# The last batch's ff stage by seven half-size products, with some masks and sums on GpSimd

## The chip, the cores and the metric

The kernel runs on one core of a Trainium2 chip. The metric is the device time of one execution in microseconds (us); lower is better. Its engines are called TensorE (PE in the profile, its weight loads PEld), VectorE (DVE), ScalarE (ACT), GpSimd (POOL) and SyncE (SP, which here issues DMAs). Each engine works through its own queue in order; semaphores order the engines among each other.

## The reference

Local attention with block summaries, then a feed-forward layer with a gelu.

```python
# q, k, v: (4, 8, 768, 64) float32; block, window = 32, 16
k_sum = k.reshape(B, H, nb, block, D).max(axis=3)
v_sum = v.reshape(B, H, nb, block, D).mean(axis=3)
scores_l = scale * q @ k^T, kept where |i - j| < window, else -1e9
scores_s = scale * q @ k_sum^T + log(block)
a = softmax(concat([scores_l, scores_s]))
attn = a @ concat([v, v_sum])
x = attn.transpose(0, 2, 1, 3).reshape(B * S, H * D)      # (3072, 512)
h = x @ w_in                                              # w_in (512, 2048)
g = h * sigmoid(1.702 * h)
out = g @ w_out                                           # w_out (2048, 512)
```

## The kernel before

The four batches go through the same stages one after the other, with the attention of a batch laid between the output products of the batch before. All matmuls are in bf16 or f16.

**Names of the order.** The whole program is one string, `ORDER` (lines 35 to 110): words with arguments, each of which calls one function (the table `ops`, line 915). A word's place sets the place of its instructions in the queue of each engine that it uses. An ending `.a`, `.d` or `.g` picks ScalarE, VectorE or GpSimd for it. `_Ordered` (line 18) wraps every engine and tells the framework after each instruction to keep it in program order; since all instructions go through it, the profile gives them all line 28.

**Attention of a batch.** `s.b.half.p` computes the scores of a half of the rows (half) and a pair of heads (p) into PSUM (`ps_s`), `e.half.p` takes the exponential on ScalarE (`a_sb`), `m.half.p` (`mask`, line 668) multiplies it by the 0/1 mask `mk` on VectorE, `v.b.half.p` multiplies it with the values (`ps_av`), `nn.half.g` normalises two pairs on VectorE (a reciprocal and a product into `x2`), and `d.half.g` turns the result by a DMA transpose on SyncE's queue into `xT` (`xTT[half][g]`). Before that, `xk` and `xq` turn keys and queries by DMA, `xa` and `ka`, `kR` fill in block maxima and halos of the keys, `vm` and `vb` sum the values by block (TensorE, then a copy and four additions on VectorE), `ha` and `sd` copy rows of values by DMA; `lk`, `lq`, `lv` load the next batch's inputs from GpSimd's queue. Batches alternate between two sets of buffers; set 0 (`kx0`, `qT0`, `vw0`, in the pool `even`) serves batches 0 and 2, set 1 batches 1 and 3.

**The ff stage.** `f.half.nt.k...` (`ff`, line 721) computes one ff tile: 128 of the 2048 ff columns for 384 of the batch's 768 rows, four matmuls over the model dimension of 512, into one PSUM bank `ph`; `g.half.nt` takes the gelu on ScalarE into `gT`. A batch has 16 x 2 such tiles.

**The output products.** They already go by seven products in place of eight (a Winograd form of Strassen's scheme): ff columns, rows and model columns are each cut in two, `ws` holds four sums of `w_out`, and `gs.j.n.what` (`g_sums`, line 740) forms four sums of `gT`, for `n` ff tiles from tile `j` on and their partners eight tiles on. `p.t.what` (`product`, line 829) is one product of eight matmuls of 256 columns, `what` in 1, 2, 6, 5, 7, 3, 4, into one of the banks `poA`, `poB`, `poC`; several of them accumulate into the same bank, and in between `x.t.what` (`taken`, line 852) copies the bank away (1, 6, 5, as `s`) or adds it to such a copy (2, 3, 7) or copies it out (4), on ScalarE or VectorE. `o` stores `osb` from SyncE's queue, three buffers of it. A product of type 5 needs the sums `gs.j.n.0` of all eight j, types 6, 7 and 3 those of kinds 1, 2 and 3.

**PSUM.** Banks 0 to 3 are single; 4 and 5 are two banks wide, whose halves are written 40, 41, 50, 51 and which are taken whole as 42 and 52.

**The same for the ff stage, not in use.** `seven_pool`, `w_sum7`, `x_sum7`, `product7`, `taken7` and `gelu7` (lines 751 to 814) are there for the ff stage; the order before has only `P7.0` near its end, which closes the pool of set 0 and makes nothing.

Of the kernel before, what the change touches and what calls it, by code (L numbers as in the profile page):

```python
# [17 lines left out]
class _Ordered:  # L18


    def __init__(self, tc, eng):
        self._tc, self._eng = tc, eng

    def __getattr__(self, name):
        f = getattr(self._eng, name)

        def call(*a, **kw):
            r = f(*a, **kw)  # L28
            self._tc.keep_in_program_order(r)
            return r  # L30

        return call
# [46 lines left out]
v.2.0.3.51 m.1.2 p.1.2.2 m.1.1 lq.3.5 p.1.7 o.1.0.0.0.2 nn.0.0 x.1.2.a o.1.0.1.0.2 m.1.3 x.1.7.a p.1.3 nn.0.1 lv.3.3.1
lq.3.7 m.1.0 p.1.4 p.2.1.2 v.2.1.0.40 v.2.1.2.50 d.0.0 v.2.1.1.41 v.2.1.3.51 x.2.5.a x.2.1.d x.1.3.a lq.3.3 p.2.6  # L80
o.1.1.0.0.2 x.1.4.d d.0.1 p.2.3 nn.1.0 x.2.6.a p.2.7 nn.1.1 p.2.2.3 x.2.7.a x.2.2.a lv.3.4.0 d.1.0 lv.3.2.1 p.2.4
f.0.9.k01.3 x.2.3.a f.0.1.k01.0 G d.1.1 o.1.2.0.0.2 f.0.1.k23 f.0.8.k01.1 f.0.8.k23 f.0.9.k23 x.2.4.a f.0.0.k01.2
f.0.0.k23 lk.3.6 g.0.1 g.0.9 g.0.8 f.1.1.k0123.0 f.1.8.k0123.1 g.0.0 f.1.9.k0123.3 g.1.1 g.1.9 g.1.8 f.1.0.k0123.2
f.0.10.k0123.0 g.0.10 gate.2 g.1.0 gs.0.2.2 xk.1.1.0 f.1.2.k0123.1 gs.0.2.0.d gs.0.2.1 xk.1.0.1 f.1.10.k0123.3 g.1.2
o.1.1.1.0.2 g.1.10 lq.3.6 f.0.2.k0123.2 gs.0.2.3 lv.3.5.1 f.1.3.k0123.1 vm.3.52 g.1.3 xk.1.1.1 g.0.2 xk.1.0.0
o.1.2.1.0.2 f.0.13.k0123.0 f.0.3.k0123.2 f.1.11.k0123.3 f.0.12.k0123.1 g.0.3 g.0.13 g.1.11 xa.0.1 f.0.4.k0123.2 xq.1.1
f.1.12.k0123.3 lq.3.1 f.0.11.k0123.0 g.0.4 gs.2.2.2.g g.0.12 f.1.5.k0123.1 g.0.11 lq.3.2 vb xa.1.1 xq.1.0 f.0.5.k0123.2
g.1.5 g.1.12 ha.3.3.0 f.1.4.k0123.0 kR.1.d g.1.4 f.1.14.k0123.3 g.0.5 f.1.6.k0123.1 g.1.14 gs.2.2.0 ha.3.1.0
# [25 lines left out]
def kernel(  # L114
# [636 lines left out]
    def seven_pool(n):  # L751
        even.close()
        if not n:
            return
        p7 = ctx.enter_context(tc.tile_pool(name="seven", bufs=2, side="right", reuse_waits="tile"))
        seven["pool"] = p7
        seven["w"] = p7.tile([128, 4, 2, n * 128], F16, name="ws7", tag="ws7", bufs=1)
        seven["x"] = p7.tile([128, 4, 2, HALF], F16, name="xs7", tag="xs7", bufs=1)

    def w_sum7(what, j0, n, eng):  # L760
        c = slice(j0 * 128, (j0 + n) * 128)
        d = slice(d_ff // 2 + j0 * 128, d_ff // 2 + (j0 + n) * 128)
        a11, a12, a21, a22 = (w_in_sb[:, 0:2, c], w_in_sb[:, 2:4, c], w_in_sb[:, 0:2, d], w_in_sb[:, 2:4, d])
        w = seven["w"][:, :, :, c]
# [10 lines left out]
    def product7(j, what, where=None):  # L775
        c = slice(j * 128, j * 128 + 128)
        d = slice(d_ff // 2 + j * 128, d_ff // 2 + j * 128 + 128)
        w, x = seven["w"], seven["x"]
        lhs, rhs, name = {
            1: (w_in_sb[:, 0:2, c], xTT[0][0], "A"),  # L780
            2: (w_in_sb[:, 2:4, c], xTT[0][1], "C"),
            6: (w[:, 1, :, c], x[:, 1], "A"),
            5: (w[:, 0, :, c], x[:, 0], "B"),
            7: (w[:, 2, :, c], x[:, 2], "A"),
            3: (w[:, 3, :, c], xTT[1][1], "B"),
            4: (w_in_sb[:, 2:4, d], x[:, 3], "A")}[what]
        opens = where is not None
        if opens:
            seven[j, name] = bank(where, F32, "ph" + name)[:, 0:HALF]
# [174 lines left out]
```

## Time and profile before

| | |
|---|---|
| median of 3 runs | 212.25 (211.74 to 213.11) |
| the profiled execution | 211.7 |
| its span, first to last instruction | 210.0 |
| moved by DMA | 27.74 MB, 132 GB/s in the mean |
| granted TensorE clock | 0.996 |

A row of a timeline has the start in us, the time until its last instruction ends, engine, line, operation, output<-input, partitions x elements and type, and how many instructions are merged in it; in brackets stands how long the engine stood idle before and for what. A row of a grouped view has the count, the busy time in us, the mean of one instruction in ns, and behind the second bar the engine's idle time before these instructions and what ended most of it.

In these terms batch 2's attention runs from about 100.8 us, its ff stage from 123.1, batch 3's attention from 144.6, batch 3's ff stage from 167.1 and the last output products from 187.9.

### The profile page before, as it was taken

The page shows a single profiled execution, that of the slowest core. Times are in us where ns is not written, and L with a number is a line of the kernel's source. Part 1 is how long each engine was busy: PE and PEld are TensorE (multiplying, and loading weights), DVE is VectorE, ACT ScalarE, POOL GpSimd, SP SyncE. Part 2 cuts the span into 40 slices and gives each one's busy share as a digit, 9 for nine tenths or more (in the row PEclk, how much of TensorE's full clock was granted, in tenths as well). Part 3 has the DMA queues.
Part 4 walks back from the last instruction along what each step waited for, and adds up shares of the span by engine and source line. Part 5 has one row for each costly group of instructions (what it writes and reads, how often), then busy time and mean ns, then how long its engine had stood idle before and what let it go on. Part 6 is the DMA issues. An engine that isn't in the chain of part 4 may idle for free.

```text
span 210.0 us, 5880 instructions
## 1 busy us (share of the span) xinstructions
PE 200.4 (95%) x2440; PEld 145.8 (69%) x2440; DVE 130.8 (62%) x311; ACT 114.3 (54%) x227; POOL 109.1 (52%) x157
## 2 busy tenths in 40 slices
PE   7998798999999999999999999999999999999993
PEld 5656554667887886556788865657888865668882
DVE  5577873798997871168997822694888500166342
ACT  2473885659666736676764336567670157671100
POOL 7999972399982998448949422431000000863000
PEclk9999999999999999999999999999999999999998
DMA  4999999999999999999999999939215920000214
GB/s 67 162 166 189 209 213 221 182 144 122 99 134 199 156 177 183 130 126 141 148 166 204 142 227 180 187 29 169 50 53 139 160 105 0 0 3 0 100 53 150
DMA packets 96458, 27.74 MB, mean 132 GB/s; under 512 B 85024, under 2 KB 93488, under 8 KB 96432
## 3 DMA queue, kind: packets, MB, share of 16 engines
q0 software_dynamic: 70800, 13.64, 82.7%
q1 hardware_dynamic: 25632, 13.74, 33.2%
q8 instruction: 19, 0.31, 0.6%
q14 instruction: 7, 0.06, 0.1%
HBM read 27.26 MB, written 6.29 MB: 160 GB/s over the span
## 4 chain that ended last, share of the span: by engine, by line
PE 79%; POOL 12%; DMA 5%; issue 1%; DVE 1%; SPq 0%; POOLq 0%; DVEq 0%
PE ph L28 36%; PE poA L28 19%; PE poB L28 10%; PE poC L28 5%; PE ps_s L28 3%; PE ps_av L28 3%; DMA vw<-vw 2%; POOL mk L28 2%; DMA out_dram<-osb 2%; POOL v0n L28 2%; POOL w_in_sb L28 2%; POOL kb L28 2%; POOL kx L28 2%; POOL qb L28 1%; PE ps_t L28 1%
## 5 line engine op out<-in xcount | busy, mean ns | idle before, releaser
L28 PE MATMUL ph<-xT,w_in_sb 128*128 128x384 f16 x512 | 86.1, 326 | 0.4 <-DVE osb L28 0.4
L28 ACT ACTIVATE gT<-ph 128x384 f16<-128x384 f32 x128 | 56.1, 495 | 30.6 <-PE ph L28 29.9
L28 PEld LDWEIGHTS <-w_in_sb 128*128 128x128 f16 x512 | 49.2, 98 | 32.4 <-issue 0.9
L28 PEld LDWEIGHTS <-gs 128*128 128x128 f16 x384 | 36.5, 98 | 4.6
L28 DVE TENSOR_TENSOR gs<-gT 128x768 f16<-128x768 f16 (+1 forms) x36 | 17.5, 498 | 29.1 <-ACT gT L28 29.0
L28 POOL TENSOR_TENSOR gs<-gs,gT 128x768 f16<-128x768 f16 (+1 forms) x6 | 8.8, 1461 | 41.8 <-PE ph L28 32.7
L28 POOL DMA_DIRECT2D kb<-in_k_dram x28 | 23.1, 842 | 13.7 <-DMA w_out_sb<-in_moe_w_out_dram 6.4
L28 ACT ACTIVATE a_sb<-ps_s 128x768 bf16<-128x768 f32 x32 | 24.8, 808 | 9.5 <-PE ps_s L28 9.3
L28 PEld LDWEIGHTS <-gT 128*128 128x128 f16 x288 | 27.3, 98 | 3.6
L28 POOL DMA_DIRECT2D vw<-in_v_dram x36 | 25.7, 752 | 5.0 <-DMA w_out_sb<-in_moe_w_out_dram 1.7
L28 PE MATMUL poA<-ws,gs 128*128 128x256 f16 x192 | 24.8, 273 | 0.0
L28 POOL DMA_DIRECT2D qb<-in_q_dram x28 | 23.8, 867 | 1.8 <-issue 0.9
L28 DVE TENSOR_TENSOR a_sb<-a_sb,mk 128x768 bf16<-128x768 bf16 x28 | 14.7, 550 | 3.0 <-ACT a_sb L28 2.2
L28 DVE TENSOR_TENSOR x<-ps_av,rc 128x768 f16<-128x768 f32 (+1 forms) x18 | 15.6, 869 | 0.6
L28 ACT ACTIVATE s<-poA 128x256 f32<-128x256 f32 x14 | 5.4, 382 | 19.3 <-PE poA L28 18.6
L28 PE MATMUL poB<-ws,gs 128*128 128x256 f16 x96 | 12.5, 273 | 0.0
L28 PE MATMUL poC<-w_out_sb,gT 128*128 128x256 f16 x96 | 12.5, 273 | 0.0
L28 PE MATMUL poA<-w_out_sb,gT 128*128 128x256 f16 x96 | 12.4, 273 | 0.0
L28 PE MATMUL poB<-w_out_sb,gs 128*128 128x256 f16 x96 | 12.4, 273 | 0.0
L28 PE MATMUL poA<-ws,gT 128*128 128x256 f16 x96 | 12.3, 273 | 0.0
L28 DVE TENSOR_REDUCE ka<-kx 128x48 bf16<-128x1536 bf16 x4 | 7.0, 1750 | 7.4 <-DMA kx<-kb 7.4
L28 ACT ACT_TABLE_LOAD x8 | 10.3, 1283 | 0.9 <-PEq L948 0.8
(102 smaller groups left out, 219.0 us busy)
## 6 DMA issues: line engine op xcount, KB each, us to landing
out_dram<-osb SPq DMA_DIRECT2D x23, 256.0 KB, 2.9
kb<-in_k_dram POOLq DMA_DIRECT2D x24, 96.0 KB, 6.0
qb<-in_q_dram POOLq DMA_DIRECT2D x24, 96.0 KB, 5.0
vw<-in_v_dram POOLq DMA_DIRECT2D x36, 64.0 KB, 5.1
w_out_sb<-in_moe_w_out_dram POOLq DMA_DIRECT2D x4, 512.0 KB, 14.8
w_in_sb<-in_moe_w_in_dram POOLq DMA_DIRECT2D x3, 512.0 KB, 11.3
vw<-vs SPq DMA_DIRECT2D x6, 198.0 KB, 3.9
kb<-in_k_dram POOLq DMA_DIRECT2D x4, 192.0 KB, 4.4
```

The source lines that it names most:

```text
L28: r = f(*a, **kw)
```

## The change

**The order.** `ORDER` is another one from batch 2's attention on (line 75 before). The counts of attention words and of output products stay; their places change, and the engines of some: three masks of batch 2 (`m.1.0`, `m.0.2`, `m.1.2`) and four of batch 3 (`m.0.0`, `m.0.3`, `m.1.0`, `m.1.1`) go to GpSimd, the halos `ka.1` too; some `gs` sums go from one to the other of VectorE and GpSimd; some `x` between ScalarE and VectorE.

**The pins.** `_Ordered` also adds, for each instruction, a dependency without a semaphore on the one before it on that engine.

**Seven products in the last ff stage.** `P7.6.2` closes the pool of set 0 once batch 2's attention is done, and opens in its place one for six pairs of ff tiles, (2, 10) to (7, 15). `W.what.2.6.d` forms four sums of `w_in` (128 x 1536 each) on VectorE during batch 2's ff stage, `U.what` four of `xT` (128 x 768 each), three on GpSimd and one on VectorE. `P.j.what` is a product of two matmuls of 384 columns (`product7`). A pair has three PSUM banks: a wide one `phX` with halves l and r, which in the end hold the left and the right half of tile j, and a single one `phA` for products 6, 7 and 4. `S.j.what` (`taken7`) copies l to `phA` after product 1 and r to the SBUF tile `r7` after product 5; after product 6 it adds `phA` and `r7` into r, in PSUM, where product 3 goes on accumulating, and after product 7 it adds `phA` to `r7`. `H.j.0`, `H.j.1` and `H.j.2` (`gelu7`) take the gelu of `phX` (both halves), `phA` and `r7`. Pairs (0, 8) and (1, 9) stay with `f` and `g`.

`w_sum` gets an engine argument that the order does not use, and `taken` takes the tiles `s1` from the pool `snap` always, as it did before in effect.

```diff
@@ _Ordered
             self._tc.keep_in_program_order(r)
+            if self._last is not None:
+                self._tc.add_manual_dep(r.ins, self._last, mybir.DependencyInfo(
+                    mybir.DependencyClass.NoSync, mybir.DependencyReason.DATA), reason="program order")
+            self._last = r.ins.name
             return r
@@ ORDER, batch 2's attention
+p.2.5.1 p.0.1.2 e.0.1 gs.7.1.1 gs.7.1.3 ha.2.3.0 x.0.1.a p.0.5.3 gs.6.1.1 gs.6.1.2.g x.0.5.a p.0.6 gs.4.2.3 ha.2.1.0
...
+e.0.2 s.2.1.1.52 lv.3.3.0 s.2.1.0.42 x.0.7.a e.1.0 m.0.0 p.0.4 x.0.3.a lq.3.0 m.1.0.g p.1.1.3 e.1.1 m.0.2.g o.1.0.0.0.2
+s.2.1.2.42 m.0.1 xk.1.0.1 x.0.4.a lq.3.4 lv.3.0.0 e.1.2 x.1.1.d s.2.1.3.52 m.0.3 p.1.2.2 x.1.5.a v.2.0.0.40 v.2.0.1.41
+p.1.6 x.1.6.a x.1.2.a m.1.2.g nn.0.0 p.1.3 p.1.7 e.1.3 x.1.3.a lq.3.5 o.1.0.1.0.2 lv.3.3.1 p.2.1.2 x.1.7.a x.2.1.d
+v.2.1.0.40 v.2.0.2.50 lq.3.7 v.2.0.3.51 d.0.0 lq.3.3 x.2.5.a m.1.1 nn.0.1 p.1.4 p.2.6 v.2.1.1.41 m.1.3 x.2.6.d
+v.2.1.2.50 v.2.1.3.51 nn.1.0 x.1.4.a o.1.1.0.0.2 p.2.3 d.0.1 p.2.2.3 p.2.7 nn.1.1 x.2.2.a f.0.9.k01.3 x.2.3.a d.1.0
@@ ORDER, the end of batch 2's ff stage and batch 3's attention
+f.1.5.k0123.1 g.1.5 f.1.15.k0123.3 gs.0.2.1 f.0.13.k0123.0 xq.1.0 o.1.1.1.0.2 g.0.13 f.0.6.k0123.2 f.1.6.k0123.1
+gs.4.2.0 f.0.15.k0123.0 g.1.15 gs.4.2.1 g.1.6 f.1.14.k0123.3 g.0.15 g.0.6 f.1.7.k0123.1 g.1.14 f.0.14.k0123.0 ha.3.1.0
+g.1.7 g.0.14 vb W.1.2.6.d o.1.2.0.0.2 gs.2.2.0.g gs.2.2.2.g gs.2.2.1.d f.0.7.k0123.2 gs.4.2.3.g ha.3.0.0 W.3.2.6.d
+gs.2.2.3 gs.6.1.0 o.1.2.1.0.2 sd.3.1.0 gs.7.1.0 ha.3.3.0 p.0.5.1 g.0.7 X s.3.0.0.52 s.3.0.1.42 p.0.1.2 gs.4.2.2.g
+p.0.2.3 e.0.1 p.1.2.0 gs.7.1.1.d x.0.5.d x.0.1.a s.3.0.3.42 gs.6.1.1 e.0.0 s.3.1.0.52 x.0.2.a gs.7.1.3 p.0.6 p.1.1.3
+gs.0.2.3 gs.6.1.3 e.1.0 x.1.1.d gs.6.1.2.g sd.3.0.0 ha.3.2.0 gs.7.1.2 e.0.3 m.0.0.g s.3.0.2.52 s.3.1.1.42 x.0.6.a e.0.2
+e.1.1 m.0.3.g p.0.7 p.0.3 s.3.1.3.42 x.0.7.a m.1.0.g m.0.1 m.0.2 s.3.1.2.52 x.0.3.a e.1.2 p.0.4 m.1.1.g e.1.3 p.1.6
...
@@ ORDER, batch 3's ff stage
+x.1.7.a nn.1.1 d.1.0 p.2.5.1 d.1.1 U.0.g U.1.g p.2.6 p.1.4 f.0.1.k01.0 G x.2.6.a x.1.4.a o.2.1.0.0.2 x.2.5.a P.3.1.52
+f.0.1.k23 P.2.1.42 p.2.2.3 p.2.3 x.2.2.a p.2.7 x.2.3.a g.0.1 f.0.8.k01.1 f.0.8.k23 U.2.d P.2.5 P.3.5 g.0.8 S.3.5.a
+f.1.1.k0123.0 S.2.5.a x.2.7.a f.1.8.k0123.1 p.2.4 g.1.1 S.2.1.a.0 g.1.8 S.3.1.a.1 P.2.6 P.2.2 P.3.2 P.3.6 f.0.9.k01.3
+S.2.6.d P.2.3 P.2.7 S.3.6.d S.2.7.d P.3.3 U.3.g P.3.7 f.0.9.k23 P.2.4 S.3.7.d x.2.4.a H.2.0 H.3.0 P.4.1.42 P.4.5 H.2.1
...
@@ mask
-    def mask(half, p):
+    def mask(half, p, eng=dve):
         a = a_sb[half, p]
-        dve.tensor_mul(a, a, mk[:, half * TH:(half + 1) * TH, :].unsqueeze(1)
+        eng.tensor_mul(a, a, mk[:, half * TH:(half + 1) * TH, :].unsqueeze(1)
                        .to_broadcast([128, 2, TH, QT]))
@@ product7
+            1: (w_in_sb[:, 0:2, c], xTT[0][0], "l"),
+            2: (w_in_sb[:, 2:4, c], xTT[0][1], "l"),
+            6: (w[:, 1], x[:, 1], "A"),
+            5: (w[:, 0], x[:, 0], "r"),
+            7: (w[:, 2], x[:, 2], "A"),
+            3: (w[:, 3], xTT[1][1], "r"),
             4: (w_in_sb[:, 2:4, d], x[:, 3], "A")}[what]
+        if where is not None:
+            X = seven[j, "X"] = bank(where, F32, "phX")
+            seven[j, "l"], seven[j, "r"] = X[:, 0:HALF], X[:, 512:512 + HALF]
         for i in range(2):
+            pe.matmul(out=seven[j, name], lhsT=lhs[:, i], rhs=rhs[:, i], start=(what in (1, 5) and i == 0),
+                      stop=(i == 1), skip_group_check=True)
@@ taken7
+        if what == 1:
+            seven[j, "A"] = bank(where, F32, "phA")[:, 0:HALF]
+            copy(eng, seven[j, "A"], seven[j, "l"])
+        elif what == 5:
+            seven[j, "h"] = seven["pool"].tile([128, HALF], F32, name="r7", tag="r7", bufs=3)
+            copy(eng, seven[j, "h"], seven[j, "r"])
         else:
+            to = seven[j, "r"] if what == 6 else seven[j, "h"]
+            eng.tensor_tensor(out=to, in0=seven[j, "A"], in1=seven[j, "h"], op=ALU.add)
```

More of the change, by code (lines that the diff above doesn't have):

```diff
@@ L79 @@
[L79 to L88, printed above, removed]
@@ L786, in product7 @@
             4: (w_in_sb[:, 2:4, d], x[:, 3], "A")}[what]
-        opens = where is not None
-        if opens:
-            seven[j, name] = bank(where, F32, "ph" + name)[:, 0:HALF]
-        seven[j, "at", what] = ph = seven[j, name]
+        if where is not None:
+            X = seven[j, "X"] = bank(where, F32, "phX")
+            seven[j, "l"], seven[j, "r"] = X[:, 0:HALF], X[:, 512:512 + HALF]
         for i in range(2):
-            pe.matmul(out=ph, lhsT=lhs[:, i], rhs=rhs[:, i], start=(opens and i == 0), stop=(i == 1),
-                      skip_group_check=True)
```

98 lines of the change are left out of this document (38 added, 60 removed).

## The prediction, made before the changed kernel was run

> **What bounds the kernel now.** I read the page's busy table first, then TensorE's timeline, then the grouped costs of the other engines, then the stretches where VectorE and GpSimd run together.
>
> ```profile
> span 210.0 us, 5880 instructions
> ## 1 busy us (share of the span) xinstructions
> PE 200.4 (95%) x2440; PEld 145.8 (69%) x2440; DVE 130.8 (62%) x311; ACT 114.3 (54%) x227; POOL 109.1 (52%) x157
> ```
>
> ```profile
> 166.23 1.04 PE L28 MATMUL poA<-ws,gT 128*128 128x256 f16 x8
> 167.10 20.96 PE L28 MATMUL ph<-xT,w_in_sb 128*128 128x384 f16 x128
> 187.90 1.04 PE L28 MATMUL poA<-w_out_sb,gT 128*128 128x256 f16 x8
> 188.77 1.04 PE L28 MATMUL poB<-ws,gs 128*128 128x256 f16 x8
> ```
>
> ```profile
> 123.10 8.61 PE L28 MATMUL ph<-xT,w_in_sb 128*128 128x384 f16 x52 [0.41 <-DVE osb L28]
> 131.64 0.60 PE L28 MATMUL ps_vs<-vw,E 64*32 64x128 bf16 x48
> 132.18 12.52 PE L28 MATMUL ph<-xT,w_in_sb 128*128 128x384 f16 x76
> 144.63 0.52 PE L28 MATMUL ps_s<-qT,kx 64*128 64x64 bf16 x24
> ```
>
> TensorE bounds it: 200.4 of 210.0 us. The last batch's ff stage is one solid block, 128 matmuls from 167.10 to 187.90, no gap: 20.80 / 128 = 0.1625 us each, four to an ff tile, 0.65 us. A product is eight matmuls, 188.77 - 187.90 = 0.87 us. In the part of the program that the change reorders, the one wait of TensorE for data is the 0.41 us before 123.10. So the change can win at most the matmuls that it removes and that wait; any new wait of TensorE is paid in full, and this block has no slack of its own to hide one.
>
> **The matmuls.** A pair of ff tiles is 2 tiles x 2 halves x 4 = 16 matmuls; by seven products it is 7 x 2 = 14, of the same width. Six pairs: 12 fewer, 12 x 0.1625 = **1.95 us won**, all on the path.
>
> **The sums of weights and of x.** Four sums of w_in (128x1536, VectorE), four of x (128x768; three on GpSimd, one on VectorE).
>
> ```profile
> L28 DVE TENSOR_TENSOR vs<-ps_vs,vpart 32x128 bf16<-32x128 f32 x12 | 3.4, 285 | 0.2
> L28 DVE COPY s<-poB 128x256 f32<-128x256 f32 x8 | 3.4, 420 | 1.7 <-PE poB L28 1.7
> L28 DVE RECIPROCAL rc<-ps_av 128x12 f32<-128x12 f32 x14 | 3.2, 228 | 3.6 <-PE ps_av L28 3.2
> L28 DVE TENSOR_TENSOR ws<-w_out_sb,ws 128x1024 f16<-128x1024 f16 x4 | 2.8, 688 | 0.5 <-DMA w_out_sb<-in_moe_w_out_dram 0.5
> L28 DVE TENSOR_TENSOR ws<-w_out_sb 128x1024 f16<-128x1024 f16 x4 | 2.7, 686 | 1.9 <-DMA w_out_sb<-in_moe_w_out_dram 1.9
> L28 DVE TENSOR_TENSOR gs<-gT,gs 128x384 f16<-128x384 f16 x7 | 2.6, 372 | 0.0
> ```
>
> ```profile
> L28 DVE TENSOR_TENSOR a_sb<-a_sb,mk 128x768 bf16<-128x768 bf16 x8 | 4.2, 551 | 0.1
> L28 DVE TENSOR_TENSOR x<-ps_av,rc 128x768 f16<-128x768 f32 x4 | 3.8, 958 | 0.1
> ```
>
> ```profile
> L28 POOL TENSOR_TENSOR gs<-gT 128x768 f16<-128x768 f16 x3 | 4.8, 1633 | 0.0
> L28 POOL TENSOR_TENSOR gs<-gs,gT 128x768 f16<-128x768 f16 x2 | 3.6, 1788 | 32.7 <-PE ph L28 32.7
> L28 POOL TENSOR_TENSOR gs<-gs,gT 128x384 f16<-128x384 f16 x1 | 0.9, 912 | 2.1 <-DVE gs L28 2.1
> ```
>
> ```profile
> 130.05 1.03 DVE L28 TENSOR_TENSOR gs<-gT 128x768 f16<-128x768 f16 x2 [6.67 <-ACT gT L28]
> ```
>
> ```profile
> DMA to landing us min/median/max: 2.7/2.8/4.3
> ```
>
> From 0.55 us at 768 and 0.69 at 1024 columns a weight sum of 1536 is an estimated 0.96 us. W.0 and W.2 fall into batch 2's ff stage, where VectorE stands idle 6.67 us: nothing. W.1 and W.3 stand late there, just ahead of gs.6.1.0 and gs.7.1.0; see the first crossing below. U.0 waits for the transpose of x's second half (landing 2.8 us after issue, the last row, from the tile view of xT), behind nn.1.0 (about 1.2 us with its reciprocal), then takes up to 1.79 on GpSimd: 5.8 us after v.3.1.1. TensorE has six products, two ff tiles and two half products (6 x 0.87 + 4 x 0.325 + 2 x 0.325 = 7.2 us) between the last value product and P.2.5, which needs U.0. U.1 to U.3 have more work ahead of their readers. Nothing, with 1.4 us to spare.
>
> **The chain inside the new stage.** Each pair evacuates four times (S.1, S.5 copies; S.6, S.7 adds) and takes three gelus.
>
> ```profile
> 168.93 0.49 ACT L28 ACTIVATE gT<-ph 128x384 f16<-128x384 f32 x1 [1.24 <-PE ph L28]
> ```
>
> ```profile
> 183.55 1.79 ACT L28 ACTIVATE gT<-ph 128x384 f16<-128x384 f32 x4 [0.16 <-PE ph L28]
> ```
>
> ```profile
> 146.76 1.49 ACT L28 ACTIVATE a_sb<-ps_s 128x768 bf16<-128x768 f32 x2
> ```
>
> The first gelu starts 0.2 us after its tenth matmul's slot (167.10 + 1.63 = 168.73). Back to back a 384 gelu costs ScalarE 0.43 us, a 768 one 0.7. ScalarE gets 8 plain gelus, 6 wide, 12 single, 8 copies: 28 x 0.43 + 6 x 0.7 = 16.2 us in a stage of 116 x 0.1625 = 18.85: busy 86%, and in order. VectorE gets 4 copies and 12 adds, about 0.55 each by the 256-column row of 0.42 quoted below, half full. Walking the three generations of two pairs by hand, TensorE is ahead of its releaser mostly at P.3.6, P.5.6, P.7.6 and the openings after a wide gelu, by 0.1 to 0.2 us each: I take **0.7 us lost**. No row shows ScalarE or VectorE writing PSUM; from 0 (all covered) to 2.0 (each of the 24 evacuations 0.3 us longer than a write to SBUF, a quarter of it exposed at TensorE).
>
> **Work moved to GpSimd.** This is where I choose.
>
> ```profile
> 185.37 0.49 DVE L28 TENSOR_TENSOR gs<-gT 128x384 f16<-128x384 f16 x1 [6.01 <-ACT gT L28]
> 185.79 2.26 DVE L28 TENSOR_TENSOR gs<-gs,gT 128x768 f16<-128x768 f16 x2
> ```
>
> ```profile
> 180.82 4.83 POOL L28 TENSOR_TENSOR gs<-gT 128x768 f16<-128x768 f16 x3
> 185.61 1.76 POOL L28 TENSOR_TENSOR gs<-gs,gT 128x768 f16<-128x768 f16 x1
> ```
>
> ```profile
> 190.72 0.42 DVE L28 TENSOR_TENSOR osb<-poC,s 128x256 f32<-128x256 f32 x1 [1.02 <-PE poC L28]
> 191.06 0.49 DVE L28 TENSOR_TENSOR gs<-gT,gs 128x384 f16<-128x384 f16 x1
> ```
>
> ```profile
> 190.43 0.91 POOL L28 TENSOR_TENSOR gs<-gT,gs 128x384 f16<-128x384 f16 x1
> ```
>
> Two VectorE sums that take about 0.9 us alone took 2.26 from 185.79, while GpSimd's sum ran from 185.61 to 187.37. The one at 185.37 slipped in between two GpSimd sums; the next, issued before that one had ended, had to let GpSimd go first. So the two engines take turns on sums that read two SBUF operands, and the one that waits, waits out the other's whole instruction. The add at 190.72 reads PSUM and one SBUF operand: 0.42, its usual time, under the GpSimd sum from 190.43. Masks, g sums and weight sums are of the first kind; evacuations, normalisation and block sums are not.
>
> The Trainium skill has this as a rule: "SBUF — State Buffer", section "Who interferes with whom", calls the pair of ports that VectorE and GpSimd share an exclusive lock, which a two-SBUF-input VectorE instruction and a GpSimd instruction that reads SBUF hold in turn. By it alone, moving masks to GpSimd would free VectorE of little and could hold it 1.6 us at a time; the rows at 185.79 and 190.72 agree.
>
> A GpSimd mask has no row; by the sums of the same size it is 1.63 us against VectorE's 0.47 (0.55 less the overlap of neighbours). Four crossings:
>
> First, the end of batch 2's ff stage. The new order runs product p.0.5.1 straight after the last ff tile; it needs gs.6.1.0 and gs.7.1.0 by its seventh and eighth matmul, 0.66 and 0.76 us in. On VectorE these stand behind gs.4.2.0, gs.4.2.1, the block sums (five small operations of 0.285, 1.4 us), W.1, gs.2.2.1, W.3, gs.2.2.3. gs.4.2.0 waits for the gelu of f.1.5, nine ff tiles (5.85 us) before the product: it starts 5.1 us before it. Alone: 4 x 0.47 + 1.4 + 2 x 0.88 + 2 x 0.29 = 5.6 us, ready 0.5 us into the product: just in time. But GpSimd now has gs.4.2.3, gs.4.2.2 (1.63 or more each) and gs.6.1.2 (0.91) in the same 5 us. The first hides behind the block sums but for 0.3; taking turns, the others add 2.5. So 0 to 2.7 us; by the row at 185.79, with a turn sometimes missed, **2.0**.
>
> Second, batch 3's attention: p.0.7 needs gs.7.1.2, on VectorE behind gs.0.2.3, gs.6.1.3 and x.1.1, while m.0.0 and m.0.3 run on GpSimd. Alone it is ready 0.4 us ahead. One turn 1.63 - 0.4 = **1.2**; bounds 0 and 2.7 (two turns, part of the second hidden).
>
> Third, batch 2's attention: v.2.1.2 and v.2.1.3 wait for nn.0.1 and m.1.3, behind m.1.1, which meets m.1.2 on GpSimd. GpSimd's masks also stand behind the loads lq.3.0, lq.3.4 and lv.3.0.0, with one to two us in hand. 0 to 0.9, **0.3**: half a turn less the cover. Against it the 0.41 wait goes.
>
> ```profile
> 122.63 0.42 DVE L28 TENSOR_TENSOR osb<-poC,s 128x256 f32<-128x256 f32 x1 [1.16 <-DMA out_dram<-osb]
> ```
>
> It came from x.2.2 finding its output buffer still being stored, and the new order takes that buffer from an earlier store: **0.41 won**.
>
> Fourth, the g sums after the new stage, five on GpSimd beside VectorE's: 0 to 0.9, **0.4**; the second half of them meets evacuations, which do not cross.
>
> The key halos moved from VectorE to GpSimd (ka.1) come ahead of lq.3.1 and lq.3.2; the loads go out about as late as before and xq.1.0 keeps its margin. The pins I price at nothing: the rows above show the engines in the written order already.
>
> Sum: -1.95 - 0.41 + 0.7 + 2.0 + 1.2 + 0.3 + 0.4 = +2.24 us. The profiled execution took 211.7 (span 210.0 and 1.7 around it), the median is 212.25, within 0.3%. On the median: **214.5**; with one or two of the crossings nearer to their lower or upper bounds, 212.3 to 216.5.
>
> **Rivals.** Cover holds: VectorE reaches gs.7.1.0 no later than 0.76 us into p.0.5.1, because its queue is served back to back and GpSimd waits instead, or GpSimd did its sums earlier. Decided at that one place; every later crossing then is the same kind. For it: alone, each chain is ready in time; the masks leave VectorE, 7 x 0.47 = 3.3 us. Against: 0.2 us of slack, and the row at 185.79. Then -1.95 - 0.41 + 0.7 = -1.7: 210.6, faster.
>
> Every turn lost: the upper bounds, -2.36 + 0.7 + 2.7 + 2.7 + 0.9 + 0.9 = +5.5: 217.8. Against it, a wait at one crossing gives VectorE time to catch up for the next.
>
> The PSUM chain: no crossing costs, but the evacuations are long: -2.36 + 2.0 = -0.4: 211.9.
>
> **How the numbers follow.** A measurement tells about 1% from no change. My forecast 0.50 (of it 0.18 within 1%, that is under 214.4), cover holds 0.30 (0.08 of it under 210.1), every turn lost 0.12, PSUM chain 0.08 (half of it with some crossings; 0.05 within 1%). Faster 0.08, within 1% 0.22 + 0.18 + 0.05 = 0.45, slower 0.32 + 0.12 + 0.03 = 0.47. The range leaves out the lower half of the second case and a third of the third: 210.5 to 217.4.
>
> **What would show it.** The ff stage: 32 plain matmuls on ph and 84 on phX and phA, about 19.6 us with waits. Before the first poB of batch 3, a wait of TensorE put down to VectorE's gs, and VectorE's W sums or g sums at 1.5 us or more under a GpSimd sum. Before p.0.7 a second. GpSimd's masks at 1.6. Wrong: no wait of TensorE there, VectorE's sums at 0.55 with GpSimd's stretched instead; or waits inside the stage put down to ScalarE's phA.

## The result, and the profile after

The changed kernel takes 223.88 us in the median of four runs (223.53 to 224.67) against 212.0 (211.42 to 213.11) before: 1.056 times the time, 95% interval 1.051 to 1.061. Some executions of a kernel come out more than 1.5% longer than its fastest one; the medians in this document are over all runs, the ratios over the others alone. The direction was forecast, the size was not: 214.5, with 217.4 as the upper end. The profiled execution took 223.97, its span is 222.3 against 210.0.

First the head of the page and its rows of busy tenths for TensorE and its clock (the changed kernel):

```profile
span 222.3 us, 5934 instructions
## 1 busy us (share of the span) xinstructions
PE 203.7 (92%) x2428; PEld 145.1 (65%) x2428; DVE 143.3 (64%) x308; ACT 121.0 (54%) x239; POOL 133.0 (60%) x174
...
PE   7897899999999999998999769993999999998994
...
PEclk9999999999999999999999979999799999999999
```

Twelve matmuls fewer, and TensorE is busy 3.3 us longer: some of its matmuls have become slower. The row of the clock says which: two of its forty slices read 7, and each stands near a slice in which TensorE idles (the 7 and 6 and the 3 of the PE row). Next, TensorE's timeline of the changed kernel from batch 2's ff stage on; only rows that the account below uses:

```profile
126.42 0.50 PE L28 MATMUL ph<-xT,w_in_sb 128*128 128x384 f16 x2 [0.54 <-DMA xT<-x]
129.61 13.21 PE L28 MATMUL ph<-xT,w_in_sb 128*128 128x384 f16 x70 [2.69 <-DMA xT<-x]
...
149.79 0.82 PE L28 MATMUL poB<-ws,gs 128*128 128x256 f16 x6
154.02 0.55 PE L28 MATMUL poB<-ws,gs 128*128 128x256 f16 x2 [3.41 <-DVE gs L28]
...
156.92 2.44 PE L28 MATMUL poC<-w_out_sb,gT 128*128 128x256 f16 x16
159.29 0.52 PE L28 MATMUL ps_s<-qT,kx 64*128 64x64 bf16 x24
...
163.42 0.28 PE L28 MATMUL poA<-ws,gs 128*128 128x256 f16 x1 [0.42 <-DVE gs L28]
...
168.35 1.03 PE L28 MATMUL poA<-w_out_sb,gT 128*128 128x256 f16 x8 [0.35 <-ACT osb L28]
```

```profile
204.08 3.10 PE L28 MATMUL poA<-ws,gs 128*128 128x256 f16 x24 [0.63 <-DVE gs L28]
207.46 1.05 PE L28 MATMUL poB<-w_out_sb,gs 128*128 128x256 f16 x8 [0.29 <-DVE gs L28]
```

And the granted clock around the two large waits, by windows (stretch, its length, then busy time and count of PE, PEld, DVE, ACT and POOL, and behind them the clock, the DMA share and GB/s):

```profile
130.00:131.00 1.00, 1.00 (x7) 0.57 (x6) 0.00 (x0) 0.87 (x3) 0.85 (x2) 0.84 0.92 138
131.00:132.00 1.00, 1.00 (x4) 0.46 (x3) 0.00 (x0) 0.38 (x1) 0.68 (x1) 0.50 0.64 74
...
134.00:135.00 1.00, 1.00 (x7) 0.63 (x6) 0.00 (x0) 0.63 (x2) 0.00 (x0) 0.95 0.51 33
...
154.00:155.00 1.00, 0.98 (x22) 0.69 (x24) 0.86 (x3) 0.00 (x0) 0.00 (x0) 0.79 0.00 0
155.00:156.00 1.00, 1.00 (x16) 0.73 (x11) 0.42 (x2) 0.66 (x1) 0.00 (x0) 0.50 0.00 0
...
157.00:158.00 1.00, 1.00 (x7) 0.69 (x6) 0.00 (x0) 0.84 (x2) 0.00 (x0) 0.51 0.00 0
```

TensorE goes on at full clock when the wait ends (1.00 in the stretch from 129 to 130), and then falls to half of it: at 130.7 behind the first wait (a mean of 0.84 in the stretch from 130 is 0.32 us at half) and at 154.6 behind the second, 1.1 and 0.6 us after TensorE went on. By the stretches in which it returns (0.95 and 0.51) it is back at 134.1 and 158.0: 3.4 us at half clock each time, which loses 1.7 us of work. The 70 matmuls from 129.61 took 13.14 us to the next row at 142.75 (not shown) where 70 x 0.1625 = 11.4 are due: 1.8 us beyond the wait itself. Between 154.02 and 159.29, 5.27 us went by with work for 3.3 (26 matmuls of 0.109 and one set of scores of 0.46): 2.0 beyond the wait. So of these 1.8 and 2.0 us the clock has 1.7 each.

The account by stages, each stage's length taken from where TensorE starts it, in us (products that the change has moved over a border are counted with their old stage, 0.87 each):

| stage | before | after | difference |
|---|---|---|---|
| up to batch 2's ff stage | 123.10 | 122.83 | -0.3 |
| batch 2's ff stage | 21.53 | 26.96 | +5.4 |
| batch 3's attention | 22.47 | 29.14 | +6.7 |
| batch 3's ff stage | 20.80 | 19.95 | -0.85 |
| last output products | 18.33 | 19.94 | +1.6 |
| behind the last product | 3.77 | 3.48 | -0.3 |
| span | 210.0 | 222.3 | +12.3 |

Of the 5.4, 3.2 are waits for `xT` and 1.8 is lost behind them, nearly all to the halved clock; of the 6.7, 3.4 are the wait inside p.0.5.1, 2.0 is lost behind it, 1.7 of that to the clock, and 0.8 are the next two waits. The rest are short lags.

### The profile page after: what moved, and what is told of

Same layout as the page of the kernel before. It is cut to its first block, busy times and chain, and to the rows that moved or that the text cites. A ratio compares the mean times of both kernels' runs of the same rounds, so it can differ in the third digit from the quotient of the medians.

```text
span 222.3 us, 5934 instructions
## 1 busy us (share of the span) xinstructions
PE 203.7 (92%) x2428; PEld 145.1 (65%) x2428; DVE 143.3 (64%) x308; ACT 121.0 (54%) x239; POOL 133.0 (60%) x174
## 5 line engine op out<-in xcount | busy, mean ns | idle before, releaser
L28 PE MATMUL ph<-xT,w_in_sb 128*128 128x384 f16 x416 | 74.2, 331 | 3.4 <-DMA xT<-x 3.2
L28 PEld LDWEIGHTS <-w_in_sb 128*128 128x128 f16 x452 | 43.8, 99 | 33.3 <-issue 6.1
L28 ACT ACTIVATE gT<-ph 128x384 f16<-128x384 f32 x104 | 46.3, 497 | 29.9 <-PE ph L28 28.7
L28 PEld LDWEIGHTS <-gs 128*128 128x128 f16 x384 | 36.2, 98 | 11.4 <-DVE gs L28 6.4
L28 PEld LDWEIGHTS <-gT 128*128 128x128 f16 x288 | 27.9, 100 | 5.1 <-issue 0.3
L28 POOL DMA_DIRECT2D kb<-in_k_dram x28 | 23.1, 840 | 11.4 <-DMA w_out_sb<-in_moe_w_out_dram 6.2
L28 POOL TENSOR_TENSOR gs<-gT 128x768 f16<-128x768 f16 (+1 forms) x8 | 12.6, 1578 | 14.4 <-ACT gT L28 14.4
L28 POOL TENSOR_TENSOR a_sb<-a_sb,mk 128x768 bf16<-128x768 bf16 x7 | 12.1, 1747 | 8.8 <-ACT a_sb L28 8.8
L28 DVE TENSOR_TENSOR a_sb<-a_sb,mk 128x768 bf16<-128x768 bf16 x21 | 13.4, 658 | 2.9 <-POOL mk L28 1.5
L28 PE MATMUL poA<-w_out_sb,gT 128*128 128x256 f16 x96 | 13.3, 285 | 0.3 <-ACT osb L28 0.3
L28 PE MATMUL poA<-ws,gT 128*128 128x256 f16 x96 | 12.3, 273 | 0.0
L28 DVE TENSOR_TENSOR gs<-gs,gT 128x768 f16<-128x768 f16 (+1 forms) x17 | 12.0, 721 | 0.2
```

## The experiments

Three theories came from this reading. **Loads:** GpSimd's masks of batch 2 hold up the loads behind them in its queue, these then run while the transposes `d` fetch x, and xT lands late. **Turns:** the wait in p.0.5.1 is VectorE's queue of sums held up by GpSimd's, as forecast; its rival is that W.1 and W.3 simply stand in the way. **Clock:** a wait of TensorE beyond some length costs the halved clock behind it as well; its rival is that what slows these matmuls is something else that happens there. Single times spread (the kernel before took 210.2 to 214.9 in 17 runs beside one group of these), so where a kernel was run once, its waits are read first and its time second.

### Loads

The answers of the tile xT, batch 2's four transposes, before and after, and GpSimd's timeline in the changed kernel:

```profile
DMA to landing us min/median/max: 3.2/4.3/5.7
```

```profile
DMA to landing us min/median/max: 5.8/6.1/7.8
```

```profile
109.72 3.55 POOL L28 TENSOR_TENSOR a_sb<-a_sb,mk 128x768 bf16<-128x768 bf16 x2 [1.39 <-ACT a_sb L28]
113.21 0.89 POOL L28 DMA_DIRECT2D qb<-in_q_dram  x1
114.10 0.70 POOL L28 DMA_DIRECT2D vw<-in_v_dram  x1
114.81 1.66 POOL L28 TENSOR_TENSOR a_sb<-a_sb,mk 128x768 bf16<-128x768 bf16 x1
...
120.95 0.87 POOL L28 DMA_DIRECT2D kb<-in_k_dram  x1
129.71 0.19 POOL L28 CAST gate<-xT 128x1 bf16<-128x1 f16 x1 [7.88 <-DMA xT<-x]
```

Three masks push the last loads out to 121.8; before, the last one ran from 116.74 to 117.6. The transposes are issued at the same times in both (113.9 to 121.7 and 114.0 to 121.3), but now share the time with loads and take 1.8 us longer in the median.

**m2_vector.** The changed kernel with batch 2's three masks back on VectorE.

```diff
-... lq.3.0 m.1.0.g p.1.1.3 e.1.1 m.0.2.g o.1.0.0.0.2
+... lq.3.0 m.1.0 p.1.1.3 e.1.1 m.0.2 o.1.0.0.0.2
...
-p.1.6 x.1.6.a x.1.2.a m.1.2.g nn.0.0
+p.1.6 x.1.6.a x.1.2.a m.1.2 nn.0.0
```

> The changed kernel with the three masks of batch 2 back on VectorE, all else as it is. Theory A: the masks hold up the input loads behind them on GpSimd's queue; the loads then share the DMA engines with the transposes of x, which land 5.8 us or more after issue (before: 4.3 in the median), so TensorE waits 3.2 us at the start of batch 2's ff stage and then runs at half its clock for some 3 us. It expects the loads 3 to 4 us earlier, landings of x at about 4.5, no wait over 0.5 us on xT there, no dip of the granted clock there, and a span 4.5 to 5.5 us shorter, 217 to 218. Rival B: the keys' transpose xk.1.0.1, moved early on SyncE's queue, and the stores delay x; it expects the wait and the dip unchanged and a span within 1 us of 222.3.

Measured 218.9, span 217.2, 5.1 shorter than the changed kernel's. The loads end at 115.6, the landing is below, no wait for xT is left and no halved clock there; the wait in p.0.5.1 is still 3.40.

```profile
DMA to landing us min/median/max: 2.8/4.1/7.6
```

This takes away masks and late loads together, so the next run takes the loads alone.

**loads_behind.** The masks stay on GpSimd; six loads that are issued among the transposes move behind the gate, where GpSimd waits for xT anyway.

```diff
-... lq.3.5 ... lv.3.3.1 ... lq.3.7 ... lq.3.3 ... lv.3.4.0 ... lv.3.2.1 ... gate.2 P7.6.2
+... gate.2 lq.3.5 lv.3.3.1 lq.3.7 lq.3.3 lv.3.4.0 lv.3.2.1 P7.6.2
```

> The changed kernel with its masks left on GpSimd, and the six loads lq.3.5, lv.3.3.1, lq.3.7, lq.3.3, lv.3.4.0, lv.3.2.1 moved behind the gate that waits for x. Theory A expects what the masks' removal gives at this place: landings of x at 3 to 4.5 us, no wait on xT over 0.5 us, no dip of the clock; the later loads may cost something at xq or at the block sums. Rival B expects the wait unchanged. Rival C, that the masks delay VectorE's normalisation through the shared port and not the loads, expects the wait unchanged too.

Measured 220.0, span 218.3, 4.0 shorter. Landing:

```profile
DMA to landing us min/median/max: 2.7/3.0/6.0
```

No wait for xT and no halved clock at the start of the stage. So it was the loads, not the masks as such. The wait in p.0.5.1 is 4.16 here, and the clock is halved for 6.8 us from within it (5.0 of them with work, so 2.5 lost in place of 1.7); these two make up for more than the 1.1 us that this kernel wins less than m2_vector.

How late xT lands is not a matter of the loads alone, though. Of the fourteen kernels of this document, five have loads beside the transposes until 121.5 or later; in all of them TensorE waits for xT at the start of the stage, 1.3 to 3.2 us. In seven of the other nine it doesn't, in no_crossing and best (below) it waits 1.1 and 1.4. The medians of the landing overlap: 5.2 to 8.1 us in the five, 3.0 to 5.9 in the nine.

**masks_alone.** The kernel before, with the same three masks on GpSimd and nothing else.

```diff
-m.0.2 ... m.1.2 ... m.1.0
+m.0.2.g ... m.1.2.g ... m.1.0.g
```

> The kernel before with only the three masks of batch 2 on GpSimd. Theory: in before's order the first of these masks comes later among the loads, two of them ahead of lq.3.5 and later loads; the loads go out about 3 us later, x lands later by 1 to 2 us and TensorE waits 1 to 3 us at the start of batch 2's ff stage, with a dip if it is over 2: 1 to 4 us more than before. Rival: masks on GpSimd are harmless by themselves and only the new order makes them costly; within 0.5 us of before.

Measured 214.91 in the median of four runs against 211.81 in the same round: 1.0147, interval 1.0091 to 1.0202. The masks alone cost some 3 us. Its profile shows two places. TensorE waits 1.27 us for xT; but the transposes are issued some 2.5 us later here than before (116.7 to 123.8), so this wait can't be put down to the loads alone. The cause of the delay is the second place, first TensorE, then VectorE, then GpSimd:

```profile
117.80 1.03 PE L28 MATMUL poA<-ws,gT 128*128 128x256 f16 x8 [1.87 <-DVE osb L28]
```

```profile
109.84 5.63 DVE L28 TENSOR_TENSOR a_sb<-a_sb,mk 128x768 bf16<-128x768 bf16 x1
```

```profile
110.73 1.66 POOL L28 TENSOR_TENSOR a_sb<-a_sb,mk 128x768 bf16<-128x768 bf16 x1
112.32 0.73 POOL L28 DMA_DIRECT2D vw<-in_v_dram  x1
113.06 1.65 POOL L28 TENSOR_TENSOR a_sb<-a_sb,mk 128x768 bf16<-128x768 bf16 x1
```

A mask of VectorE that takes 0.55 alone took 5.63: two GpSimd masks that started after it ended before it, and all that stands behind it on VectorE, the output adds among them, was late. In the changed kernel the VectorE mask in the same place got through in 0.76. These runs do not let one foresee which of the two happens.

### Turns

VectorE's and GpSimd's timelines of the changed kernel before p.0.5.1, from 145.26 and 143.16:

```profile
145.26 1.87 DVE L28 TENSOR_TENSOR gs<-gs,gT 128x768 f16<-128x768 f16 x1
...
148.58 1.15 DVE L28 TENSOR_TENSOR ws<-ws,w_in_sb 128x1536 f16<-128x1536 f16 x1
149.66 1.98 DVE L28 TENSOR_TENSOR gs<-gs,gT 128x768 f16<-128x768 f16 x1
151.57 1.66 DVE L28 TENSOR_TENSOR ws<-w_in_sb,ws 128x1536 f16<-128x1536 f16 x1
153.15 0.55 DVE L28 TENSOR_TENSOR gs<-gT,gs 128x768 f16<-128x768 f16 x1
```

```profile
143.16 3.56 POOL L28 TENSOR_TENSOR gs<-gT 128x768 f16<-128x768 f16 x2 [4.55 <-ACT gT L28]
147.28 1.64 POOL L28 TENSOR_TENSOR gs<-gT,gs 128x768 f16<-128x768 f16 x1 [0.56 <-DVE gs L28]
148.88 3.53 POOL L28 TENSOR_TENSOR gs<-gT 128x768 f16<-128x768 f16 x2
```

Each stretched VectorE sum ends just after a GpSimd sum does, and the first one after GpSimd's last sum takes 0.55 again. Against 0.55 for a sum and 0.96 for W (as g4_vector below shows it) the four stretched ones cost 1.32 + 0.19 + 1.43 + 0.70 = 3.6 us; TensorE's wait is 3.4.

**g4_vector.** The changed kernel with gs.4.2.3, gs.4.2.2 and gs.6.1.2, the three GpSimd sums that the first crossing was priced by, on VectorE and later, behind gs.7.1.3.

```diff
-f.0.7.k0123.2 gs.4.2.3.g ha.3.0.0 ... p.0.1.2 gs.4.2.2.g p.0.2.3 ... gs.7.1.3 p.0.6 ... x.1.1.d gs.6.1.2.g sd.3.0.0
+f.0.7.k0123.2 ha.3.0.0 ... p.0.1.2 p.0.2.3 ... gs.7.1.3 gs.4.2.2 gs.4.2.3 gs.6.1.2 p.0.6 ... x.1.1.d sd.3.0.0
```

> The changed kernel with W.1 and W.3 where they are, late, and only the three GpSimd g sums that met them (gs.4.2.3, gs.4.2.2, gs.6.1.2 of batch 2) moved to VectorE, behind gs.7.1.3 of batch 3's attention. VectorE's work ahead of p.0.5.1 is the same as in the change; what goes is the other engine. Theory of turns: the sums W.1, gs.2.2.1 and W.3, which took 1.15, 1.98 and 1.66 us, go back to about 0.95, 0.55 and 0.95; that is 2.3 us, the wait at p.0.5.1 falls from 3.4 to 0.8 to 1.4 us and the dip goes. Rival, that VectorE just has too much ahead of that product: the wait stays over 2.5 us.

Measured 222.97, span 221.3: only 1.0 won. TensorE's rows at the two crossings:

```profile
149.89 0.55 PE L28 MATMUL poB<-ws,gs 128*128 128x256 f16 x2 [1.06 <-DVE gs L28]
...
161.52 0.28 PE L28 MATMUL poA<-ws,gs 128*128 128x256 f16 x1 [4.26 <-DVE gs L28]
```

In front of p.0.5.1 the wait fell from 3.41 to 1.06, the W sums took 0.96 and 0.95, gs.2.2.1 0.56, and no halved clock followed. gs.4.2.1 still took 1.88, beside gs.2.2.0 and gs.2.2.2 on GpSimd, which the prediction had not counted. But the sums now stand on VectorE ahead of gs.7.1.2, and there they met batch 3's masks on GpSimd:

```profile
156.06 3.69 DVE L28 TENSOR_TENSOR gs<-gT,gs 128x768 f16<-128x768 f16 x2
```

So p.0.7 waits 4.26, and the half clock moved behind it. The turns are paid where two-input work of both engines meets, wherever that is put.

**w_early.** The changed kernel with W.1 and W.3 right behind W.2, where VectorE is idle.

```diff
-... W.2.2.6.d f.0.12.k0123.1 ... vb W.1.2.6.d o.1.2.0.0.2 ... ha.3.0.0 W.3.2.6.d gs.2.2.3
+... W.2.2.6.d W.1.2.6.d W.3.2.6.d f.0.12.k0123.1 ... vb o.1.2.0.0.2 ... ha.3.0.0 gs.2.2.3
```

> The changed kernel with W.1 and W.3 straight behind W.2, at the start of batch 2's ff stage, where VectorE is idle for 12 us. Theory: at p.0.5.1 the weight sums and the turns taken with GpSimd's g sums make TensorE wait 3.4 us; without the two, 2.8 us of VectorE's time (1.15 and 1.66, waits for GpSimd in them) leave the chain, the wait falls to 0.6 to 1.2 us, the clock does not dip behind it (2.0 us), and the span falls by 4 to 5 us to 217.5 to 218.5. Rival: GpSimd's sums only fall on the other g sums instead and the wait stays over 2.5 us with its dip; span within 1 us of 222.3. The wait on xT stays in both.

Measured 220.0, span 218.3, 4.0 shorter; the waits were

```profile
127.12 15.09 PE L28 MATMUL ph<-xT,w_in_sb 128*128 128x384 f16 x82 [2.88 <-DMA xT<-x]
151.68 0.55 PE L28 MATMUL poB<-ws,gs 128*128 128x256 f16 x2 [1.67 <-DVE gs L28]
```

The first has its halved clock, the second none. With the W sums out of the way 1.7 us of p.0.5.1's wait is gone, not the 1.15 + 1.66 that they took: GpSimd's sums still hold up two of VectorE's (1.88 and 1.87 in its timeline). Both theories have their share: the W sums in the path, and GpSimd's turns.

**m3_vector.** The changed kernel with batch 3's four masks on VectorE (`m.0.0`, `m.0.3`, `m.1.0`, `m.1.1`, without the ending `.g`).

> The changed kernel with the four masks of batch 3 back on VectorE, all else as it is. It prices the second crossing: 0.42 us before p.0.7 and 0.35 before v.3 in the changed kernel. Theory: both waits go, no more than 0.8 us of TensorE's time; the waits on xT and at p.0.5.1 stay with their dips. Rival: the masks hold up more than shows as waits; over 1.5 us less between 154 and 175 us.

Measured 222.84, span 221.1, 1.2 shorter: the waits of 0.42 at p.0.7 and 0.35 behind it are gone, p.0.5.1's is 3.41 as before. The second crossing was real and small.

### Clock

**wait_short** and **wait_long.** The kernel before, with one mask of batch 3 (0/1, so that repeating it changes nothing) done five and ten times on VectorE, to make TensorE wait where before it does not.

```diff
-p.0.4 p.1.7 m.1.0 x.0.4.a
+p.0.4 p.1.7 m.1.0 m.1.0 m.1.0 m.1.0 m.1.0 x.0.4.a
```

> The kernel before with the mask m.1.0 of batch 3 done five times over on VectorE (the mask is 0 or 1, so nothing changes in the result): 4 x 0.47 = 1.9 us more ahead of the normalisation nn.0.1 and of v.3.1.0. It measures what a wait of TensorE costs beyond its length. Theory: a wait of 1 to 1.5 us near 161 us, no dip of the granted clock behind it (no wait under 2 us has had one so far), and a span longer by the waits alone, 1 to 2 us. Rival: any wait dips the clock.

> The same with m.1.0 ten times: 9 x 0.47 = 4.2 us more. Theory: a wait of 3 to 3.6 us, then the granted clock at 0.5 for 3 to 3.5 us, which costs another 1.6 to 1.8 us; span 5 to 6 us longer than before. Rival: the dips after the waits of 2.7 and 3.4 us in the changed kernel have another cause (the DMA, or the kind of work); the clock stays at 1.0 here and the span grows by 3 to 4 us.

wait_short took 214.17, wait_long 218.06. TensorE's rows, first of the short, then of the long one, and the clock of the long one:

```profile
161.46 1.03 PE L28 MATMUL poB<-w_out_sb,gs 128*128 128x256 f16 x8 [1.11 <-DVE s L28]
162.33 1.04 PE L28 MATMUL poA<-ws,gT 128*128 128x256 f16 x8
```

```profile
163.23 1.87 PE L28 MATMUL poB<-w_out_sb,gs 128*128 128x256 f16 x8 [4.06 <-DVE s L28]
164.89 1.91 PE L28 MATMUL poA<-ws,gT 128*128 128x256 f16 x8
```

```profile
161.00:162.00 1.00, 0.00 (x0) 0.00 (x0) 0.93 (x4) 0.00 (x0) 0.00 (x0) 0.64 0.00 0
...
168.00:169.00 1.00, 1.00 (x18) 0.87 (x15) 0.67 (x2) 0.00 (x0) 0.00 (x0) 0.95 0.91 359
```

A wait alone does it, without seven products, masks on GpSimd or a DMA that is late. Behind the short one, products start every 0.87 us as ever; behind the long one, every 1.66. Here the clock falls within the wait, at 161.3, and is back at 168.1: 6.8 us, twice as long as in the changed kernel and as I had expected. 4.9 us of it had work, which cost 2.4. So the lengths are not all the same, and the price of a long wait is not one figure. (Both kernels' traces have a halved clock early on too, from 24.8 and 21.3 us; that is far ahead of the edit and plays no part in these rows.)

### What the seven products are worth

**hybrid.** The order of before up to batch 3's ff stage, with the four W sums in batch 2's ff stage, and the changed kernel's order from there.

```diff
 (the order before, to nn.1.1 of batch 3; in batch 2's ff stage:)
+P7.6.2 W.0.2.6.d W.2.2.6.d W.1.2.6.d W.3.2.6.d g.0.1
 (then the changed order:)
+d.1.0 d.1.1 U.0.g U.1.g f.0.1.k01.0 x.2.6.a o.2.1.0.0.2 x.2.5.a P.3.1.52 f.0.1.k23 P.2.1.42 ...
```

> The order of before up to batch 3's ff stage, masks on VectorE; all four weight sums at the start of batch 2's ff stage; from batch 3's ff stage on the order of the change, seven products with it. It shows what the seven products are worth alone. Theory: the ff stage at 19.6 to 20.0 us against 20.8, no wait on xT and none at the first product; behind the stage the g sums still cross, 1.0 to 1.6 us. Together minus 1.0 plus 1.3: 0.0 to 0.8 us more than before, 211.8 to 213.2. Rival: the seven products are themselves what costs (PSUM chains, sums of x), and the kernel stays over 216.

Ten runs, 212.84; ratio 1.0039 (0.9995 to 1.0083). In its profile, waits of 0.62 and 0.29 for g sums stand behind the new stage, as in the changed kernel: the fourth crossing. The stage itself, counted as in the table, takes 20.4 us here and in hybrid_sums, where 19.6 to 20.0 was expected: 0.4 less than the 20.80 before, which is too little for ten runs to tell. TensorE also waits 1.24 us for an `osb` at the start of batch 2's ff stage (0.41 before).

**hybrid_sums.** The same, with the four g sums of GpSimd behind the last ff pairs on VectorE, and the `x` copies that VectorE had there on ScalarE.

```diff
-gs.6.1.1.g ... gs.6.1.2.g ... x.0.6.d gs.7.1.3.g ... gs.6.1.3.g ... x.0.4.d ... x.1.6.d ... x.2.6.d
+gs.6.1.1 ... gs.6.1.2 ... x.0.6.a gs.7.1.3 ... gs.6.1.3 ... x.0.4.a ... x.1.6.a ... x.2.6.a
```

> As hybrid, but behind the last ff stage the four small g sums (gs.6.1.1, gs.6.1.2, gs.7.1.3, gs.6.1.3) on VectorE in place of GpSimd, and three copies of products on ScalarE in place of VectorE. Theory: the waits there (0.6, 0.4 and 0.3 us) come from turns with GpSimd; they fall under 0.4 together and the kernel gains 0.8 to 1.2 us on hybrid, 211.6 to 212.0. Rival: VectorE is simply full there; the four sums cost it 1.1 us more and the waits stay or grow, 212.8 or more.

Ten runs, 211.91 against 211.55: ratio 1.0008 (0.9972 to 1.0043). The two waits behind the stage are gone. Its profiled execution has a span of 208.7, 1.3 less than that shown of before, but the runs do not bear out a gain.

**no_crossing.** The changed order with every crossing taken out at once: all masks on VectorE, W early, the sums moved as in g4_vector, and behind the last stage the engines of hybrid_sums.

> The changed kernel with its order, but all seven masks on VectorE, W.1 and W.3 at the start of batch 2's ff stage, the three g sums of batch 2 that met them (gs.4.2.3, gs.4.2.2, gs.6.1.2) on VectorE behind gs.7.1.0 and gs.7.1.3, and the last sums as in hybrid_sums. Theory: all that the change lost is these crossings, the loads behind the masks and the dips of the clock; what stays is the seven products, less 0.8 us in the stage, and the 0.4 us wait that the order does away with: no wait over 1 us on TensorE, no dip, 210.5 to 212.0. Rival: the new order has losses of its own that the crossings hide; over 213.

Ten runs, 213.52; ratio 1.0082 (1.0044 to 1.012). Of the 5.6% that the changed kernel lost, 0.8% is left; the time is still 1.5 us above the upper end that I had expected. Its profile has the waits that are left, in TensorE's timeline:

```profile
108.06 0.61 PE L28 MATMUL poA<-ws,gs 128*128 128x256 f16 x4 [0.93 <-DVE gs L28]
123.81 1.15 PE L28 MATMUL ph<-xT,w_in_sb 128*128 128x384 f16 x6 [0.47 <-DMA xT<-x]
125.20 1.03 PE L28 MATMUL poA<-ws,gT 128*128 128x256 f16 x8 [0.24 <-DVE osb L28]
128.79 11.54 PE L28 MATMUL ph<-xT,w_in_sb 128*128 128x384 f16 x70 [0.60 <-DMA xT<-x]
```

All lie in batch 2's attention and at the start of its ff stage. The loads are over at 116.9, so it isn't they that make xT late here. The transposes are issued from 115.7 to 122.9, later than before; that VectorE is late with the masks back on it is the likely reason, but it isn't shown: m2_vector has the same masks on VectorE and no wait for xT.

**best.** hybrid_sums with two of batch 2's first ff tiles, f.0.9 and f.0.8, moved behind f.0.1 and f.0.0, because the banks of the former wait for the copies x.2.2 and x.2.3.

```diff
-p.2.4 f.0.9.k01.3 x.2.3.a f.0.1.k01.0 ... f.0.1.k23 f.0.8.k01.1 f.0.8.k23 f.0.9.k23 x.2.4.a f.0.0.k01.2 f.0.0.k23
+p.2.4 x.2.3.a f.0.1.k01.0 ... f.0.1.k23 x.2.4.a f.0.0.k01.2 f.0.0.k23 f.0.9.k01.3 f.0.9.k23 f.0.8.k01.1 f.0.8.k23
```

> hybrid_sums with the first ff tiles of batch 2 in another order: those two whose banks wait for x.2.2 and x.2.3, which wait for a store of 2.9 to 4.4 us, come third and fourth. Theory: the wait of 0.2 to 1.2 us at that place is covered by 1.3 us of other matmuls; 0.5 to 1.0 us less than hybrid_sums, 210.8 to 211.4, ratio to before 0.995 to 0.999. Rival: the transposes of x become what is waited for there, no gain.

Twelve runs, 211.92 against 211.81: ratio 0.9987 (0.9943 to 1.0031). In its profiled execution, one of its longer ones at 212.76, TensorE waits 1.40 us for xT there. No version was measurably faster than the kernel before.

## Why the prediction was right and wrong

**The new ff stage** was right: predicted about 19.6 us with waits, measured 19.95, so the chain of evacuations and gelus lost 1.1 where 0.7 was taken. In this kernel a write to PSUM takes about as long as one to SBUF: ScalarE's copies take 0.47 us into phA and 0.49 into r7, VectorE's adds 0.56 into phX (the row below, the mean in ns behind the bar) and 0.55 into r7. So the rival of long evacuations had no ground.

```profile
L28 DVE TENSOR_TENSOR phX<-phA,r 128x384 f32<-128x384 f32 x6 | 3.4, 563 | 4.2 <-PE phX L28 3.0 <-ACT gT L28 1.0
```

**The turns** were right as a mechanism, and each named place shows one: the wait before the seventh matmul of p.0.5.1 put down to VectorE's gs, W and g sums of 1.15 to 1.98, a second wait at p.0.7, GpSimd's masks at 1.75 in the mean. Their sizes:

- First crossing, priced 2.0 with 2.7 as the upper bound, measured 3.4. The three sums that were counted are worth 3.41 - 1.06 = 2.35 by g4_vector. What failed is "gs.4.2.0 ... starts 5.1 us before it. Alone: ... just in time", which let gs.4.2.0 and gs.4.2.1 run undisturbed: gs.4.2.1 lost a turn (1.32) to gs.2.2.0 and gs.2.2.2, which GpSimd does there too. That is of the size of the other 1.06; no run took it away.
- Second, priced 1.2: 0.4 at p.0.7 and 0.35 behind it, 1.2 of the span by m3_vector's single run. As the prediction said of a lost turn, the wait ahead of it had given VectorE time to catch up.
- Third, priced 0.3: the stage as a whole came out 0.3 earlier, with the wait of 0.41 gone, so 0.1 or so. By masks_alone it could have been 1.9: the small price here is luck of how the masks fell, not something that the prediction had shown.
- Fourth, priced 0.4 with 0.9 as the bound: the last products took 1.6 longer, 0.9 of it as two waits for g sums. That is the upper bound for the waits; the lags around them were left out.

**Two terms were not in the sum at all,** and they make most of the miss. The step that failed first is "GpSimd's masks also stand behind the loads lq.3.0, lq.3.4 and lv.3.0.0, with one to two us in hand". It looks at what stands ahead of the masks and not at what they push back: lq.3.5, lv.3.3.1, lq.3.7, lq.3.3 and others go out 4.2 us later, beside the transposes of x. That was 3.2 us of waits; loads_behind and m2_vector show it from both sides. The kernel before had the row for it: the last load at 116.74 and the transposes at 114.0 to 121.3 stood in one timeline.

The second step is the price of a wait, "any new wait of TensorE is paid in full". It is paid in full and more: two of the waits were followed by 1.8 and 2.0 us of loss, 1.7 of each by the halved clock. wait_long shows that the wait alone does this, wait_short that a short one does not. The Trainium skill states it in "TensorE: Matmul & The Clock Gate", section "HAM oscillation — how this bites in real kernels": TensorE should have no idle gaps beyond about 3.4 us, or its clock is halved. The rows here agree in kind, but waits of 2.69 and 2.88 were enough, while 2.37 (in g4_vector, before its matmuls at 129.51) was not. Had the prediction set the first crossing at its bound of 2.7, it would have stood on that edge.

With the measured sizes, the sum goes: -0.85 for the stage, 3.2 + 1.8 for the loads and their clock, 3.4 + 2.0 for the first crossing, 0.8 for the second, 1.6 for the fourth: 12.0 of the 12.3. By the stage and the turns' waits alone (-0.85 + 3.4 + 0.8 + 1.6) it would be 5.0, which makes 217, inside the range that was given: it is the two terms left out, 3.2 + 1.8 and 2.0, that carry the time beyond it.

**The pins,** priced at nothing, are not set apart from the rest by any run. hybrid_sums and best have them and are level with the kernel before (1.0008 and 0.9987), so a large price is ruled out, not a small one.

## What to carry to other kernels

When work is moved to an engine whose queue also issues loads, list what stands behind it there and what those loads will then run beside; in the changed kernel three masks cost more by the loads that they pushed back (5.0 us with the clock) than by their turns in that place (0.1 or so). Price a single wait of TensorE by its length up to 2.4 us, and add 1.5 to 2.5 where it is 2.7 or more: these runs have none in between. By these prices, splitting or filling one long wait is worth more than shortening a short one. Two-input sums on VectorE and GpSimd at the same time hold each other up, so a gain of 1 us on TensorE is easily lost when such sums are added to a stretch in which both engines already have theirs.

## What the runs showed of the hardware

- VectorE and GpSimd do not strictly take turns. By the start times in the profile, VectorE's mask in masks_alone began at 109.84, ahead of GpSimd's at 110.73, and two of GpSimd's masks with the issue of a load between them went first (5.63 us); in w_early another took 4.12, and ended 1.7 us after GpSimd's second mask, with only issues of loads running on GpSimd in between. Why it was not let in between is open. "SBUF — State Buffer" in the Trainium skill, section "Who interferes with whom", says that issue order decides who blocks; these two rows do not fit that.
- Around the long waits the halved clock lasts 3.4 us or twice that: 3.4 in the changed kernel (130.7 to 134.1, 154.6 to 158.0), and in m2_vector, g4_vector, w_early and m3_vector; 6.8 in loads_behind (147.7 to 154.5) and wait_long (161.3 to 168.1). It costs half of the part that has work: 1.7 us when it begins behind the wait; where it begins within the wait, 1.5 in w_early (127.1 to 130.0 with work), 2.5 and 2.4 in the two long ones.
- Waits of 2.69 us and more were each followed by it or ran into it (2.69, 2.88, 3.10, 3.40, 3.41, 4.06, 4.16, 4.26); single ones of 2.37 and less from batch 2's attention on were not (1.11, 1.27, 1.40, 1.67, 1.87, 2.37 among them). A long wait is not the only thing that brings it, though: between 21 and 29 us, in the first batch, where TensorE has several waits close together, none of them above 0.93 us, four of the fourteen traces show it as well, for 3.4 us (g4_vector from 22.2, no_crossing and wait_short from 24.8) or 6.8 (wait_long from 21.3). What decides there is open.
- DMA transposes that are issued at the same times as before landed 1.8 us later in the median with GpSimd's loads beside them, and 1.3 earlier with these loads moved away (medians of 4.3 before, 6.1 after, 3.0 in loads_behind). Over all runs the medians overlap (see Loads), so these differences aren't the price of the loads alone.
